# One set of spreading products for two attention blocks, and a closing barrier moved ahead of the last projections

## The chip, the cores and the metric

The kernel runs on one core of one Trainium2 chip. Its engines are named as in the profile: PE (TensorE, matrix products; PEld are its weight loads), DVE (VectorE), ACT (ScalarE), POOL (GpSimd) and SP (Sync). The metric is the device time of one execution in microseconds. The six runs of before that stand beside the changed kernel's agree within 0.14% (1321.99 to 1323.73). Two numbers are kept apart: the *time* of a run, which is the metric, and its *span*, from the first to the last instruction of the program. The time is longer than the span, by 1.3 to 1.5 us in most runs of before, and here that difference turns out to matter. All runs quoted are listed as fast; a few of them are one to two us longer than the rest, and they are named where they occur.

## The reference, cut to what matters

Two decode-attention blocks, each for one query token, are computed and their outputs laid side by side. Block A has 32 heads with 32768 keys of its own for each head; block B has 32 query heads on 8 key/value heads and looks at the last 4096 keys only.

```python
q = (x @ wq).reshape(B, Sq, H, Dh)...                 # x is one row of 512
scores = jnp.einsum("bhqd,bhkd->bhqk", q, k_cache) * (Dh ** -0.5)
p = softmax(scores)
o = jnp.einsum("bhqk,bhkd->bhqd", p, v_cache)
out = o.reshape(B, Sq, H * Dh) @ wo                   # wo is 4096 x 512
# a: all 32768 keys, 32 KV heads;  b: last 4096 keys, 8 KV heads, each for 4 query heads
return jnp.concatenate([a, b], axis=-1)
```

Nearly all the bytes are A's key and value caches, 256 MiB each in bf16, and each is read once.

## The kernel before

The program is recorded as a list of operations for each engine and then emitted inside one block. The block ends with a barrier of all five engines. Behind it the Sync engine waits for the two output stores.

```python
def build(self):
    ...
    with nc.Block() as block:                  # its end is a barrier of all five engines
        block.gpsimd(self.emit("pool"))
        block.vector(self.emit("dve"))
        block.scalar(self.emit("act"))
        block.sync(self.emit("sp"))
        block.tensor(self.emit("pe"))
    for n in self.X:
        nc.sync.wait_ge(self.outsem[n], 16)    # both outputs have landed
```

B is computed first, then A's 32 heads in a loop. "Spreading" means normalising a block's 32 x 128 attention outputs and turning them, with four small products, into the 128 x 32 layout that the output projection takes as its weights.

```python
def plan(self):
    ...
        self.emit_PV("B", g)
    self.emit_spread("B")                      # B's spread, before A's loop
    for g in range(NQH):
        ...                                    # A: load, transpose, scores, softmax, PV
    ...                                        # load_wo: the last loads, wo of B and A in pieces
    self.emit_spread("A")
    self.emit_proj()

def emit_spread(self, name):
    ...
    ri = self.op("dve", ... reciprocal(t["rinv"], ps[0:32, DH:DH + 1]), self.gath)
    ob = self.op("dve", ... tensor_scalar_mul(t["ob"], ps[0:32, 0:DH], t["rinv"]), ri)
    def mm(e):
        for dq in range(4):
            inst = e.matmul(p2[:, 0:32], lhsT=self.spread[:, 128 * dq:128 * dq + 128],
                            rhs=t["ob"][:, 32 * dq:32 * dq + 32], ...)
        return inst
    o = self.op("pe", mm, ob, self.k_sel)
    t["ozop"] = self.op("dve", ... tensor_copy(t["oz"], p2[:, 0:32]), o)
```

A's wo is loaded in six pieces of 11, 8, 6, 4, 2 and 1 rows (`WO_CUTS`), so that the last piece to land leaves little work. `emit_proj` does B's projection, sums its four strips on DVE and ACT, stores B's output, does A's projection piece by piece, evicts it in two halves (DVE and ACT) and stores A's output.

## Time and profile before

| what | before |
|---|---|
| time, 3 runs | 1322.05 us (1322.04 to 1322.24) |
| span | 1320.81 us |
| DMA moved, mean rate | 570.59 MB, 432 GB/s |
| last piece of wo landed | 1318.85 us |
| A's output store issued | 1319.70 us |
| store's semaphore complete | 1320.79 us |
| closing barrier released | 1320.36 to 1320.42 us |

The profile of before is of one more run, of 1323.17 us, which is one of the long ones: its span is that of the others, but it spent 2.36 us outside the span, where the usual is 1.3.

The page of before, first its totals, then the row of DMA in 40 slices (tenths of full business), then its queue table (packets, MB, share of the 16 engines):

```profile
span 1320.8 us, 28798 instructions
PE 968.0 (73%) x13248; PEld 677.4 (51%) x13248; DVE 753.3 (57%) x1342; ACT 56.4 (4%) x170; POOL 2.7 (0%) x22
...
DMA  9999999999999999999999999999999999999998
...
q1 hardware_dynamic: 13060, 570.43, 99.9%
q8 instruction: 8, 0.13, 0.0%
```

DMA is the limit from beginning to end. PE and DVE have time to spare everywhere but behind the last load. The end of the chain of waits of before (start, length, what) says what that last stretch is:

```profile
1288.46 29.46 DMA kbuf<-in_A_wo_dram
1317.92 0.04 issue
1317.97 1.22 PE psPT L718 x13
1319.18 0.02 issue
1319.20 0.41 DVE out_sb L725
```

And the tail of before in the timeline (start, length, engine, line, what; in brackets the engine's idle time ahead of it and what ended it):

```profile
1309.88 0.41 PE L682 MATMUL psG<-oc_A,hw 128*32 128x128 f32 x2 [1.64 <-DVE oc_A L671]
1310.32 0.16 DVE L692 RECIPROCAL rinv_A<-psG 32x1 f32<-32x1 f32 x1 [0.50 <-PE psG L682]
...
1311.24 1.90 PE L730 MATMUL psS<-kbuf,oz_B 128*1 128x512 bf16 x32
...
1314.82 1.04 PE L718 MATMUL psPT<-kbuf,oz_A 128*1 128x256 bf16 x16 [0.48 <-DMA kbuf<-in_A_wo_dram]
...
1316.73 0.82 PE L718 MATMUL psPT<-kbuf,oz_A 128*1 128x256 bf16 x12 [0.87 <-DMA kbuf<-in_A_wo_dram]
...
1317.97 1.21 PE L718 MATMUL psPT<-kbuf,oz_A 128*1 128x256 bf16 x14 [0.42 <-DMA kbuf<-in_A_wo_dram]
...
1319.20 0.41 DVE L725 CAST out_sb<-psPT 1x256 bf16<-1x256 f32 x1 [2.56 <-PE psPT L718]
...
1319.70 0.25 SPq L762 DMA_DIRECT2D out_dram<-out_sb  x1
```

The first row is the last product of A's loop, called the last gather below. Three times PE stands idle until a piece of wo has landed. A tail that starts later eats these idle times first.

The barrier is not among these rows, because semaphore instructions do not count as busy, but the trace has its records (start in us; a drain is the instruction with which an engine arrives at the barrier):

```
before   1318.90 PE drains      1319.22 DVE, 1319.25 ACT drain   1320.00 Sync drains (after its store's issue)
         1320.24 GpSimd gathers 1320.36 Sync released            1320.44 Sync waits for the store
         1320.79 store's semaphore complete                      1320.81 end of the wait = end of the span
```

So before's closing barrier runs while the store is under way.

### The profile page before, as it was taken

The page shows a single profiled execution, that of the slowest core. Times are in us where ns is not written, and L with a number is a line of the kernel's source. Part 1 is how long each engine was busy: PE and PEld are TensorE (multiplying, and loading weights), DVE is VectorE, ACT ScalarE, POOL GpSimd, SP SyncE. Part 2 cuts the span into 40 slices and gives each one's busy share as a digit, 9 for nine tenths or more (in the row PEclk, how much of TensorE's full clock was granted, in tenths as well). Part 3 has the DMA queues.
Part 4 walks back from the last instruction along what each step waited for, and adds up shares of the span by engine and source line. Part 5 has one row for each costly group of instructions (what it writes and reads, how often), then busy time and mean ns, then how long its engine had stood idle before and what let it go on. Part 6 is the DMA issues. An engine that isn't in the chain of part 4 may idle for free. (4 is left out here: it accounts for less than half of the span.)

```text
span 1320.8 us, 28798 instructions
## 1 busy us (share of the span) xinstructions
PE 968.0 (73%) x13248; PEld 677.4 (51%) x13248; DVE 753.3 (57%) x1342; ACT 56.4 (4%) x170; POOL 2.7 (0%) x22
## 2 busy tenths in 40 slices
PE   4675678777667877777787767778776767877687
PEld 3453445555444555444455544455554445555454
DVE  3563556665455666545566654566655546665564
ACT  0000000000000000000000000000000000000000
POOL 0000000000000000000000000000000000000000
PEclk8886888887788888778988887898888789888888
DMA  9999999999999999999999999999999999999998
GB/s 404 434 435 432 441 431 435 437 431 435 435 435 437 431 435 439 429 437 437 429 437 439 429 435 439 429 435 439 429 439 437 427 441 435 429 439 435 429 439 371
DMA packets 13359, 570.59 MB, mean 432 GB/s; under 512 B 1570, under 2 KB 1700, under 8 KB 2084
## 3 DMA queue, kind: packets, MB, share of 16 engines
q1 hardware_dynamic: 13060, 570.43, 99.9%
q8 instruction: 8, 0.13, 0.0%
q10 hardware_dynamic: 288, 0.00, 0.0%
q14 instruction: 3, 0.02, 0.0%
HBM read 570.43 MB, written 0.00 MB: 432 GB/s over the span
## 5 line engine op out<-in xcount | busy, mean ns | idle before, releaser
L556 DVE COPY kt<-psT 128x1024 bf16<-128x1024 bf16 x1056 | 656.2, 684 | 238.1 <-PE psT L552 236.3
L552 PE MATMUL psT<-ident,kbuf 128*128 128x128 bf16 x8448 | 582.3, 235 | 167.8 <-DMA kbuf<-in_A_k_cache_dram 154.2
L552 PEld LDWEIGHTS psT<-ident,kbuf 128*128 128x128 bf16 x8448 | 542.7, 107 | 260.0 <-DMA kbuf<-in_A_k_cache_dram 162.3
L655 PE MATMUL psACC<-vbuf,ptsb 128*4 128x512 bf16 (+1 forms) x2112 | 185.4, 527 | 22.8 <-ACT ptsb L630 22.0
L575 PE MATMUL psS<-kt,qw 128*32 128x512 bf16 x2048 | 158.3, 386 | 14.7 <-DVE kt L556 14.7
L669 DVE TENSOR_SCALAR oc_A<-psACC,hot_A 128x128 f32<-128x128 f32 x32 | 11.2, 351 | 249.9 <-PE psG L682 249.9
L655 PEld LDWEIGHTS psACC<-vbuf,ptsb 128*4 128x4 bf16 (+1 forms) x2112 | 59.4, 111 | 139.1 <-issue 91.0
L603 ACT ACTIVATE psb<-psS,nb_A 128x512 bf16<-128x512 f32 x32 | 22.0, 687 | 1168.0 <-DVE nb_A L602 1168.0
L575 PEld LDWEIGHTS psS<-kt,qw 128*32 128x32 bf16 x2048 | 34.1, 95 | 57.4 <-DVE kt L556 30.6
L682 PE MATMUL psG<-oc_A,hw 128*32 128x128 f32 (+1 forms) x128 | 19.3, 227 | 52.3 <-DVE oc_A L671 52.3
L682 PEld LDWEIGHTS psG<-oc_A,hw 128*32 128x32 f32 x128 | 11.4, 109 | 62.5 <-DVE oc_A L671 55.0
L627 PE MATMUL psPT<-ident,psb 128*128 128x128 bf16 x136 | 18.0, 275 | 34.0 <-ACT psb L603 34.0
L671 DVE SCALAR_TENSOR_TENSOR oc_A<-psACC,hot_A,oc_A 128x128 f32<-128x128 f32 x96 | 33.7, 351 | 3.4
L592 DVE TENSOR_REDUCE tr_in<-psS 128x1 f32<-128x512 f32 x34 | 23.5, 692 | 17.8 <-PE psS L575 17.8
L627 PEld LDWEIGHTS psPT<-ident,psb 128*128 128x128 bf16 x136 | 10.2, 117 | 37.0 <-ACT psb L603 36.7
L596 PE MATMUL psACC<-rows,tr_in 128*1 128x64 f32 x64 | 8.8, 220 | 25.6 <-DVE tr_in L592 25.6
L630 ACT ACTIVATE ptsb<-psPT 128x512 bf16<-128x512 bf16 x34 | 20.3, 597 | 31.1 <-PE psPT L627 31.1
L596 PEld LDWEIGHTS psACC<-rows,tr_in 128*1 128x1 f32 x64 | 2.7, 81 | 35.7 <-DVE tr_in L592 35.7
L600 PE MATMUL psACC<-mr_A,nscale 1*128 1x1 f32 x64 | 12.3, 259 | 9.8 <-DVE mr_A L599 9.8
L600 PEld LDWEIGHTS psACC<-mr_A,nscale 1*128 1x128 f32 x64 | 9.6, 186 | 15.8 <-DVE mr_A L599 15.8
L602 DVE COPY nb_A<-psACC 128x1 f32<-128x1 f32 x32 | 5.1, 158 | 15.2 <-PE psACC L600 15.2
L599 DVE TENSOR_REDUCE mr_A<-psACC 1x1 f32<-1x64 f32 x32 | 6.8, 213 | 11.8 <-PE psACC L596 11.8
(78 smaller groups left out, 71.7 us busy)
## 6 DMA issues: line engine op xcount, KB each, us to landing
kbuf<-in_A_k_cache_dram SPq DMA_DIRECT2D x4, 4096.0 KB, 22.6
kbuf<-in_B_k_cache_dram SPq DMA_DIRECT2D x2, 4096.0 KB, 31.7
vbuf<-in_B_v_cache_dram SPq DMA_DIRECT2D x2, 4096.0 KB, 25.1
vbuf<-in_B_wq_dram SPq DMA_DIRECT2D x1, 4096.0 KB, 12.4
vbuf<-in_A_wq_dram SPq DMA_DIRECT2D x1, 4096.0 KB, 32.0
kbuf<-in_B_wo_dram SPq DMA_DIRECT2D x2, 2048.0 KB, 32.2
kbuf<-in_A_wo_dram SPq DMA_DIRECT2D x1, 1408.0 KB, 25.2
kbuf<-in_A_wo_dram SPq DMA_DIRECT2D x1, 1024.0 KB, 27.3
```

The source lines that it names most:

```text
L552: inst = e.transpose(T[:, 128 * k:128 * k + 128], src[:, DH * k:DH * k + DH], self.ident[:, :])
L556: self.copies.append(self.op("dve", lambda v: v.tensor_copy(KT[:, :], T[:, :]), o, to="pe"))
L575: inst = e.matmul(self.S[32 * c:32 * c + 32, :], lhsT=win, rhs=self.kt[(bb + c // 2) % NKT][:, 512 * (c % 2):512 * (c % 2) + 512], start=b ...
L592: o = dve(lambda v: v.reduce_max(tr["in"][:, 0:1], self.S[:, :], axis=AXX), self.sdone, self.k_pool, to="pe" if name == "A" else None)
L596: o = self.op("pe", lambda e: e.matmul(self.ACC[0:1, 0:64], lhsT=tr["in"][:, 0:1], rhs=self.rows64[:, :], start=True, stop=True, skip_grou ...
L600: o = self.op("pe", lambda e: e.matmul(self.ACC[:, 64:65], lhsT=self.nscale[:, :], rhs=t["mr"][0:1, :], start=True, stop=True, skip_group_ ...
L603: self.sread = self.op("act", lambda s: s.activation(out=self.psb[:, :], in_=self.S[:, :], func=ACTF.Exp, bias=t["nb"][:, k:k + 1], scale= ...
L627: inst = e.transpose(PT[:, 128 * jj:128 * jj + 128], self.psb[:, 128 * jj:128 * jj + 128], self.ident[:, :])
L630: self.ptread = self.op("act", lambda s: s.activation(out=self.ptsb[:, :], in_=PT[:, 0:512], func=ACTF.Copy), self.psread, to="pe")
L655: inst = e.matmul(acc[32 * c:32 * c + rows, 0:512], lhsT=lhsT, rhs=rhs, start=begin, stop=end, tile_position=(0, 32 * c), skip_group_check ...
L671: o = self.op("dve", lambda v, src=src, hot=hot: v.scalar_tensor_tensor(out=oc, in0=src, scalar=hot, in1=oc, op0=ALU.mult, op1=ALU.add), p ...
L682: return self.op("pe", lambda e: e.matmul(self.G[0:32, c0 + c:c0 + c2], lhsT=win, rhs=t["oc"][g % len(t["oc"])][:, c:c2], start=False, sto ...
```

## The change

The intent is twofold. B is only normalised before A's loop; one set of four spreading products, 64 columns wide, then does both blocks at the end, which saves four products and a copy. And the operations behind the loop ("tail") are emitted after the block, so that its barrier stands ahead of the last projections instead of behind them. Cut to its core:

```diff
     def build(self):
...
             block.tensor(self.emit("pe"))
+        for eng, e in dict(pe=nc.tensor, dve=nc.vector, act=nc.scalar, sp=nc.sync).items():
+            self.rest[eng](e)
         for n in self.X:
             nc.sync.wait_ge(self.outsem[n], 16)
...
     def emit(self, eng):
-        ops = self.prog[eng]
+        ops = [o for o in self.prog[eng] if not o.tail]
+        tail = [o for o in self.prog[eng] if o.tail]
...
+            self.rest[eng] = lambda e: straight(e, tail, seen, base)
...
-        self.emit_spread("B")
+        self.emit_norm("B")
...
-        self.emit_spread("A")
+        self.tail = True
+        self.emit_spread()
         self.emit_proj()
...
+    def emit_spread(self):
+        ob, p2 = self.ob, self.T[0]
+        o = self.emit_norm("A")
         def mm(e):
             for dq in range(4):
-                inst = e.matmul(p2[:, 0:32], ..., rhs=t["ob"][:, 32 * dq:32 * dq + 32],
+                inst = e.matmul(p2[:, 0:64], ..., rhs=ob[:, :].rearrange("p (n x) -> p n x", n=2)[:, :, 32 * dq:32 * dq + 32],
...
-        deps = (self.wosem[name][part], 16), self.c[name]["ozop"]
+        deps = (self.wosem[name][part], 16), self.ozop
```

A consequence: B's projections, which needed nothing of A, now wait for A's normalisation, products and copy.

## The prediction

> **What bounds the kernel.** DMA. The queue table gives 99.9% of the span of 16 DMA engines to the load queue (570.43 MB, 432 GB/s); the 40-slice rows show DMA at 9 tenths in all slices but the last. PE is busy 73% and DVE 57%. The chain that ended last confirms it: 29.46 us of DMA for the last pieces of A's output weights (the last lands at 1318.85), then 1.22 us of last products (line 718), 0.41 us of DVE eviction, and the output store, issued from 1319.70 to 1319.95. The span ends at 1320.81. So only the 2 us behind the last landing can be won.

> **What stands at that end.** The barrier's records are in the trace, though not in the busy rows: engines drain (PE 1318.90, DVE and ACT by 1319.68, SP 1320.00 to 1320.21), GpSimd gathers at 1320.24, all are released by 1320.44. Sync then waits for the store's semaphore, which comes at 1320.79, 1.09 us after its issue (the other store took 1.13 us). The closing barrier is thus already hidden under the store. [...]

> **What the change removes.** B's spread: 4 products, 1 copy and their semaphores, about 1 us of PE and DVE before A's loop, with DMA saturated: worth 0. The barrier between store issue and final wait: the wait still ends with the store: worth 0 to 0.1 us.

> **What it adds and moves.** The barrier now sits between loop and tail. PE is its last arrival: its loop-end branch is done at 1311.0, then a branch and a drain, then 0.2 us from last gather to release (as at the end of before). I estimate the reciprocal at 1311.6 instead of 1310.32. B's projections, which started at 1311.24, must now also wait for A's normalisation, products and copy: about 1312.8 (estimate, +1.5 us). PE's work behind that, by issue times of before: B 1.4 to 1.5 us, A's first 22 products 1.3, next 16 0.75; PE is level at about 1316.4, just before the third A piece lands (1316.69). PE sat idle for DMA 0.48, 0.87 and 0.42 us ahead of these pieces; that slack absorbs the delay. Summing B's strips ends near 1318.2 instead of 1316.65, before DVE's last eviction at 1319.20; B's store lands near 1319.3, before A's. Nothing of this reaches the critical path.

> **Prediction.** 1322.0 us, 8 in 10 between 1321.6 and 1322.5. Faster by over 2%: 0.003; within 2%: 0.99; slower by over 2%: 0.007. If it moves at all, I expect under 0.3 us.

> **What the profile would show.** Right: DMA saturated, last landing within 0.3 us of 1318.9; the first tail DVE instruction about 1.3 us later against the loop's end; PE's idle for DMA shrunk or gone before the second and third A piece, still there before the last; 1.1 us from last store issue to final wait. Wrong: PE's last product well after the last landing (delay not absorbed), or a span end under 1.0 us after the last store's issue (barrier was on the path).

> **What would make it wrong.** [...] Time outside the span: other engines finish earlier and could shorten what follows. A DMA rate that differs between runs.

## The result

| | before | changed |
|---|---|---|
| time, median of 6 runs | 1322.05 us (1321.99 to 1323.73) | 1322.36 us (1322.26 to 1323.24) |
| span of the profiled run | 1320.81 us | 1320.67 us |

The ratio is 1.0001 with a 95% interval of 0.9988 to 1.0014: the same at 2%. The prediction of 1322.0 (1321.6 to 1322.5) held. The medians differ by 0.31 us, a hair more than the "under 0.3 us" that it allowed. Leaving out the one long run of each side (1323.73 and 1323.24), all runs of the changed kernel (1322.26 to 1322.52) lie above all runs of before (1321.99 to 1322.24), although the profiled span is a little shorter. That is small, but it is a question.

The page of the changed kernel:

```profile
span 1320.7 us, 28789 instructions
PE 966.1 (73%) x13244; PEld 675.0 (51%) x13244; DVE 751.7 (57%) x1341; ACT 56.4 (4%) x170; POOL 2.7 (0%) x22
...
DMA  9999999999999999999999999999999999999998
...
q1 hardware_dynamic: 13060, 570.43, 99.9%
```

Four products and one DVE instruction are gone, as planned, and DMA is as full as it was. The end of its chain of waits:

```profile
1286.73 31.65 DMA kbuf<-in_A_wo_dram
1318.38 0.04 issue
1318.42 0.62 PE psPT L731 x5
1319.04 0.02 issue
1319.06 0.41 DVE out_sb L738
```

The same three steps end the program. Its tail in the timeline:

```profile
1307.73 0.41 PE L689 MATMUL psG<-oc_A,hw 128*32 128x128 f32 x2 [1.64 <-DVE oc_A L678]
1309.20 0.16 DVE L696 RECIPROCAL rinv_A<-psG 32x1 f32<-32x1 f32 x1 [1.52 <-PEq L102]
...
1310.48 2.70 PE L743 MATMUL psS<-kbuf,oz 128*1 128x512 bf16 x32 [0.41 <-DVE oz L712]
...
1312.95 3.17 PE L731 MATMUL psPT<-kbuf,oz 128*1 128x256 bf16 x38
...
1316.54 0.82 PE L731 MATMUL psPT<-kbuf,oz 128*1 128x256 bf16 x12 [0.41 <-DMA kbuf<-in_A_wo_dram]
...
1317.77 1.25 PE L731 MATMUL psPT<-kbuf,oz 128*1 128x256 bf16 x14 [0.41 <-DMA kbuf<-in_A_wo_dram]
...
1319.06 0.41 DVE L738 CAST out_sb<-psPT 1x256 bf16<-1x256 f32 x1 [2.39 <-PE psPT L731]
...
1319.55 0.25 SPq L775 DMA_DIRECT2D out_dram<-out_sb  x1
```

From PE's last gather to the reciprocal it is now 1.47 us (1309.20 - 1307.73) instead of 0.44, with the releaser "PEq L102", the barrier. From there to B's first product it is 1.28 us (1310.48 - 1309.20) instead of 0.92. B's products take longer too: 2.70 us against 1.90 (the granted clock was 0.57 in 1311 to 1314 us against 1.00, see below). And the idle time ahead of the piece of 16 products is gone: the 38 products at 1312.95 run through. But ahead of the last two groups PE still waits 0.41 us for DMA each time, so nothing of the delay has come through. The loop also ended 2.15 us earlier in this execution than in the trace of before (1307.73 against 1309.88); the control below, the same kernel as before, has its last gather at 1308.17, so this varies between runs of one kernel.

### The profile page after: what moved, and what is told of

Same layout as the page of the kernel before. It is cut to its first block, busy times and chain, and to the rows that moved or that the text cites. A ratio compares the mean times of both kernels' runs of the same rounds, so it can differ in the third digit from the quotient of the medians.

```text
span 1320.7 us, 28789 instructions
## 1 busy us (share of the span) xinstructions
PE 966.1 (73%) x13244; PEld 675.0 (51%) x13244; DVE 751.7 (57%) x1341; ACT 56.4 (4%) x170; POOL 2.7 (0%) x22
## 3 DMA queue, kind: packets, MB, share of 16 engines
q1 hardware_dynamic: 13060, 570.43, 99.9%
HBM read 570.43 MB, written 0.00 MB: 432 GB/s over the span
```

## The experiments

Twelve kernels were run, with runs of before in between. All gave correct results. "Extra" below is time minus span of a run, which comes from the list of single runs (spans are listed to 0.1 us).

### Control and the two halves of the change

The control is before itself. Of the two halves, spread_only is one line away from the changed kernel, and barrier_only is before with the changed kernel's tail machinery (not repeated here) and that same line:

```diff
 # spread_only: the changed kernel without the tail
-        self.tail = True
```

```diff
 # barrier_only: before with the tail machinery
+        self.tail = True
         self.emit_spread("A")
```

> The kernel before, unchanged, as a control: it gives the spread of two equal kernels in the same rounds, and its own time outside the span. Both theories: ratio to before 1.0000 within 0.0002 (0.3 us), span 1320.6 to 1320.9 us, time minus span as in the other kernels (the changed kernel showed 1.6 us in all its runs).

> The changed kernel, unchanged. Theory (the change is off the critical path; the 0.3 us between the medians of the first measurement is spread or the chip): within 0.3 us of the control, span 1320.6 to 1320.9. Rival (the change costs 0.3 us outside the span, in what follows the last instruction): again 0.2 to 0.4 us above the control, at the same span, with a larger time minus span.

> The one set of spreading products for both blocks, without the move of the barrier: one line taken from the changed kernel. Theory: within 0.3 us of the control, because DMA is saturated where B's products are saved and B's projections, which must now wait for A's spread, start only 0.4 to 0.6 us later with 1 us and more of slack ahead of the last pieces. Rival (if the 0.3 us of the changed kernel is real): 0 if the barrier carries it, +0.3 us if the merged spread does.

> The barrier ahead of the tail, with B's spread where it was in the kernel before. Theory: within 0.3 us of the control; the reciprocal comes about 1.2 us later against PE's last gather, and the last products still start within 0.1 us of the last landing. Rival (if the 0.3 us of the changed kernel is real): +0.3 us if the barrier carries it, 0 if the merged spread does.

| kernel | median time, 5 runs | spans | extra, median |
|---|---|---|---|
| before in the same rounds (9 runs) | 1322.17 | 1320.7 to 1321.1 | 1.32 |
| before_again | 1322.06 | 1320.6 to 1320.8 | 1.36 |
| after_again | 1322.49 | 1320.7 to 1321.5 | 1.66 |
| spread_only | 1322.55 | 1320.7 to 1320.9 | 1.75 |
| barrier_only | 1322.15 | 1320.6 to 1321.0 | 1.25 |

My theory, that the 0.3 us were spread, fell. The 95% intervals of the four ratios, some 0.0028 wide, do not separate the kernels, but the extra does: run by run, spread_only has 1.67 to 1.78 us and after_again 1.59 to 1.69; before has 1.30 to 1.50 and barrier_only 1.22 to 1.40, each with one run at 2.4 to 2.5 that is dealt with in the last section. The halves add up: the merged spread costs about 0.4 us outside the span, the moved barrier saves about 0.1 us outside the span, and the sum is the +0.3 us of the changed kernel. Inside the span both are worth nothing, as predicted.

The trace shows where. Around the end of the span and behind it, it records steps of semaphore 2, which no instruction of the kernel touches: nine steps, then 228 to 249 other semaphores updated once each, then nine steps. In us from the end of the span:

```
                first nine steps                                       last nine steps
before_again   -0.16 -0.13 0.08 0.12 0.15 0.25 0.28 0.32 0.37     1.16 1.19 1.23 1.27 1.30 1.40 1.44 1.47 1.52
spread_only    -0.15 -0.12 0.09 0.13 0.16 0.26 0.29 0.33 0.37     1.16 1.20 1.24 1.28 1.30 1.80 1.84 1.87 1.92
barrier_only   -1.44 -1.09 -1.05 -1.01 0.12 0.16 0.20 0.23 0.28   1.07 1.10 1.14 1.19 1.21 1.31 1.35 1.38 1.43
after_again    -1.44 -1.09 -1.05 -1.01 0.12 0.16 0.20 0.23 0.28   1.07 1.11 1.15 1.19 1.21 1.71 1.75 1.78 1.83
```

The records do not say which engine makes a step. As I read them, the first nine go on as the five engines end their streams: with the barrier moved four of them come 1.44 to 1.01 us ahead of the span's end, for the other engines (in the trace of the changed kernel at 1319.24 to 1319.67, where PE's last product ends at 1319.03 and the evictions at 1319.47), and only Sync is waited for, so the nine are through 0.28 us behind the span instead of 0.37. That is the 0.1 us. With the merged spread, one of the last nine steps (the sixth) comes 0.49 or 0.50 us behind the fifth instead of 0.10. That is the 0.4 us.

### Which engine's instruction stream carries the 0.4 us

The merged spread takes four instructions from PE's stream and one from DVE's. Each was put back by itself, with work whose result nobody reads:

```diff
 # after_pe4                                     # after_dve1
-        self.emit_norm("B")                     +        pad = ...alloc_sbuf_tensor("pad", [128, 32], BF16)
+        o = self.emit_norm("B")                 +        self.op("dve", lambda v: v.tensor_copy(pad[:, :],
+        self.op("pe", pad, o, self.k_sel)       +                self.ident[:, 0:32]), self.k_ident)
 # pad: B's four old products into an unread corner of PSUM
```

> The changed kernel with B's four old spreading products put back on PE, their result unread; so PE has as many instructions as in before, DVE one fewer. So far: kernels with the merged spread spend 1.6 to 1.75 us outside the span, those without 1.25 to 1.35, and the records behind the span show one gap of 0.5 us in place of 0.1 [...]. Theory P (what counts is how many instructions PE's stream has, thus where its end code lies): time minus span falls back to 1.25 us, the gap to 0.1 us, the median to about 1322.0. Theory D (DVE's stream): stays at 1.65 us. Theory M (something about the merged spread itself): stays at 1.65 us. Span 1320.6 to 1320.9 in all.

> The changed kernel with one unused DVE copy put in where B's copy of the spread was; DVE has as many instructions as in before, PE four fewer. Theory P (PE's stream): time minus span stays at 1.65 us, median about 1322.4. Theory D (DVE's stream): falls to 1.25 us, median about 1322.0. Theory M: stays.

| kernel | PE, DVE instructions against before | median time | spans | extra, median (range) | fifth to sixth step |
|---|---|---|---|---|---|
| after_pe4 | 0, -1 | 1322.51 | 1320.7 to 1321.1 | 1.67 (1.61 to 1.77) | 0.49 |
| after_dve1 | -4, 0 | 1322.27 | 1320.7 to 1321.3 | 1.27 (1.21 to 1.29) | 0.10 |
| before, same rounds (9 runs) | 0, 0 | 1322.44 | 1320.8 to 1321.2 | 1.38 | |

Theory D it is. One DVE instruction of no use, put in ahead of A's loop, takes the 0.4 us away again. So it is neither the merged product nor PE's stream, but DVE's stream. That what counts is where this stream ends is inferred, because only one added instruction at one place was tried. Other kernels have other DVE counts with the barrier moved: +1 (after_late2) gave an extra of 1.39 us, +2 (barrier_late2) gave 1.52, +7 (after_late8) gave 1.22. That is no trend, as one would expect of a position and not of an amount of work. With +2 the sixth step is on time (0.10 us); there an 8 KB packet, which the profile lists under the kind "instruction", moves behind the span and ends last (more on this under "More barriers"). The four traces in which DVE has two or more instructions more than before, barrier instructions counted, have such an 8 KB packet in their last 2 us or behind the span, and the other ten have none, which points at a position too. What exactly delays the sixth step is not shown. One trace (four more barriers, below) has DVE pausing between two bare barrier instructions, 0.51 us from its release to its next drain against 0.11 us in the barriers before it, with nothing to wait for; the size fits, the cause stays open.

### How much slack the tail has

Two or eight DVE copies were put ahead of the reciprocal, which makes the whole tail later. I had estimated 0.7 us for each; in the traces the reciprocal came 1.2 us later with two of them (1312.15, where the first copy starts at 1310.94) and 4.8 us later with eight:

```diff
 # after_late2, after_late8, barrier_late2: in the tail, ahead of A's normalisation
+        for i in range(2):                      # 8
+            self.op("dve", lambda v, i=i: v.tensor_copy(self.kt[4 + i % 4], self.T[3] as bf16))
```

> The changed kernel with two unneeded DVE copies of 0.68 us between the barrier and the reciprocal: the whole tail behind the barrier comes 1.4 us later. Theory (the tail is off the critical path; PE has 1 to 3 us of slack before the last landing, depending on when the loop ends and which clock is granted): span up by 0 to 0.3 us. Rival (the tail is on the path): span up by 1.4 us.

> The same with eight such copies: the tail comes 5.7 us later. Theory: the slack is used up and the rest surfaces, span up by 2.5 to 4.5 us, and PE no longer waits for any of the last pieces. Rival (the tail is on the path): up by 5.7 us. Rival (these steps never matter): 0.

> The barrier moved, B's spread left where it was, and the same two needless DVE copies as in after_late2 between barrier and reciprocal. Theory S (the merged spread takes the slack: B's projections wait for A's whole spread, and all traces with it show the clock at half for 3.4 to 6.9 us inside the tail, the three without it at full): span up by 0 to 0.3 us here, against 1.3 to 1.6 us in after_late2. Rival L (the slack is lost because the loop itself ended 1.7 us later in that run): up by 1 us or more here too.

| kernel | spans, 4 runs | before in the same rounds |
|---|---|---|
| after_late2 | 1322.1, 1322.1, 1322.3, 1322.4 | 1320.8 to 1321.2 |
| after_late8 | 1323.8, 1324.7, 1325.0, 1326.2 | 1320.8 to 1321.2 |
| barrier_late2 | 1320.7, 1320.8, 1320.8, 1320.9 | 1320.6 to 1320.9 |

My expectation for after_late2 was wrong and the rival's was right: 1.2 us of delay raised the span by 1.2 us (from a median of 1321.0 to one of 1322.2). So in these four runs the changed kernel's tail had no slack to speak of, although its first trace shows PE waiting for DMA. With eight copies, 4.8 us of delay cost 2.8 to 5.2 us against the same median (3.85 in the median, as expected, but one run lies above my range); what was absorbed varies by 2.4 us among four runs. And barrier_late2, with the same delay but B's spread done early, pays nothing in any of its four runs. So with the barrier moved and B's spread left in its place there were at least 1.2 us of slack, and in the four runs of after_late2 there were not. The two ran on different chips, and no run excludes the chip as a rival.

The two timelines, after_late2 first:

```profile
1309.47 0.41 PE L689 MATMUL psG<-oc_A,hw 128*32 128x128 f32 x2 [1.63 <-DVE oc_A L678]
...
1313.42 3.56 PE L747 MATMUL psS<-kbuf,oz 128*1 128x512 bf16 x32 [0.41 <-DVE oz L716]
1316.78 3.68 PE L735 MATMUL psPT<-kbuf,oz 128*1 128x256 bf16 x64
...
1320.99 0.25 SPq L779 DMA_DIRECT2D out_dram<-out_sb  x1
```

```profile
1308.05 0.41 PE L689 MATMUL psG<-oc_A,hw 128*32 128x128 f32 x2 [1.64 <-DVE oc_A L678]
...
1311.51 3.58 PE L739 MATMUL psS<-kbuf,oz_B 128*1 128x512 bf16 x32
...
1314.88 4.30 PE L727 MATMUL psPT<-kbuf,oz_A 128*1 128x256 bf16 x64
...
1319.71 0.25 SPq L771 DMA_DIRECT2D out_dram<-out_sb  x1
```

In after_late2 all 64 of A's products run without a wait for DMA, and the last starts at 1320.19, while the last piece had landed at 1318.79: PE, not DMA, sets the end. B's first product comes 3.95 us behind the last gather (1313.42 - 1309.47) against 3.46 us (1311.51 - 1308.05), so the merged spread accounts for 0.49 us of the difference. The other 1.42 us is that A's loop ended later in this run. The spans of all four runs of after_late2 agree, so I cannot call that chance, nor did any run show a reason for it; how the slack splits between merged spread and loop end stays open. In the 14 traces the last gather starts between 1307.08 and 1309.88 us, and it is as late as here (1309.47) or later in before, before_plus1_barriers and quarters_barrier too.

A second thing had not been in the prediction: the granted clock. The stretches of 3 us in the tail (PE busy, PEld, DVE, ACT and POOL busy, then the clock, DMA share, GB/s), first of before, then of spread_only:

```profile
1311.00:1314.00 3.00, 2.94 (x56) 1.78 (x58) 0.88 (x2) 0.08 (x1) 0.00 (x0) 1.00 0.99 416
1314.00:1317.00 3.00, 1.65 (x30) 0.88 (x26) 2.04 (x3) 1.10 (x2) 0.00 (x0) 1.00 0.99 406
```

```profile
1311.00:1314.00 3.00, 3.00 (x32) 1.08 (x26) 0.15 (x1) 0.00 (x0) 0.00 (x0) 0.50 0.99 417
1314.00:1317.00 3.00, 3.00 (x42) 2.06 (x38) 2.28 (x4) 1.18 (x2) 0.00 (x0) 0.67 0.98 400
```

### More barriers at the end of before

```diff
 # before_plus1_barriers, before_plus4_barriers
             block.tensor(self.emit("pe"))
+        for _ in range(1):                      # 4
+            with nc.Block():
+                pass
```

> The kernel before with one more empty barrier behind its closing one, ahead of the wait for the store; one barrier takes 0.35 to 0.45 us from Sync's drain to release. Theory (the closing barrier is hidden under the store, which lands 0.35 us after the release): span up by 0 to 0.15 us. Rival (the barrier is on the path): up by 0.35 to 0.45 us.

> The same with four more barriers. Theory: the first is hidden, the rest surfaces: span up by 4 x 0.4 minus 0.35, so 1.0 to 1.4 us, and the final wait ends at once when it starts. Rival (each is on the path): up by 1.4 to 1.8 us.

| kernel | median time, 4 runs | spans | extra, median |
|---|---|---|---|
| before, same rounds (9 runs) | 1322.14 | 1320.6 to 1320.9 | 1.38 |
| before_plus1_barriers | 1322.80 | 1320.6 to 1321.1 | 1.97 |
| before_plus4_barriers | 1324.19 | 1322.1 to 1322.3 | 1.94 |

In the span the expectation held both times: one more barrier is still hidden under the store (the trace has Sync released from it at 1320.71 and the store complete at 1320.81), and of four more 1.4 us come through. The second is partly luck: one of the four took 0.78 us from release to release, with DVE's pause in it, against 0.33 to 0.36 us for the other three. But the time of before_plus1_barriers rose by 0.66 us, nearly all of it in the extra. So "hidden under the store" was only half right: Sync waits for the store in any case, but the other four engines have to get through the barrier before their streams end, and that shows outside the span. In the records the first nine steps end 0.70 us behind the span instead of 0.37, which is 0.33 us, just what the added barrier takes from release to release. The other 0.3 us fits a record of DMA: an instruction packet of 8 KB moved from 1.75 to 2.20 us behind the span, later than the last step at 1.83. Over all 14 traces the extra of the profiled run follows from what comes last. In eleven it is the last step's time less 0.16 to 0.19 us. In the three where an instruction packet ends later (before, barrier_late2 and before_plus1_barriers, at 2.65, 1.81 and 2.20 us) it is that packet's end less 0.29 us (2.36, 1.52 and 1.91). The extra barrier also says why moving the barrier gains only 0.1 us: it ended early enough that the other engines were late by only that much.

### A version meant to beat both

```diff
 # quarters_barrier: barrier_only with A's projection in four strips of 128 columns
-            inst = e.matmul(bank[64 * i:64 * i + 1, 0:256], ..., rhs=rhs[:, 256 * i:256 * i + 256], ...)   # i = 0, 1
+            inst = e.matmul(bank[32 * i:32 * i + 1, 0:128], ..., rhs=rhs[:, 128 * i:128 * i + 128], ...)   # i = 0..3
-        out, src = self.out_sb[0:1, 256 * i:256 * i + 256], bank[64 * i:64 * i + 1, 0:256]
+        out, src = self.out_sb[64 * i:64 * i + 64, :], bank[64 * i:64 * i + 64, 0:128]
-        e.dma_start(self.out[0, :, 0:512], self.out_sb[:, :])
+        e.dma_start(self.out[0, :, 0:512].rearrange("a (c x) -> (a c) x", c=4), self.out_sb[0:128:32, :])
```

> A version meant to beat both: barrier moved, B's spread as in before, and A's last products in four strips of 128 columns in place of two of 256, so that DVE and ACT each evict 128 columns (estimate from 0.41 us for 256 and 0.69 us for 512 columns: 0.28 us) and the store takes four pieces of 256 B. Theory: span down by 0.1 to 0.15 us and 0.1 us less outside it, median about 1321.9 against 1322.1 to 1322.4 of before. Rival (the store of four pieces takes longer to be received, or the smaller products start more slowly): no gain. A gain under 0.15 us can drown in the runs' spread; then the trace's steps from the last landing to the end decide.

It did not beat them: a median of 1322.50 us against 1322.14, spans of 1321.1, 1321.2, 1321.2, 1322.7 and 1322.8 us. The profiled run is one of the two long ones; its end in the timeline, and its line of instruction packets:

```profile
1318.44 0.28 PE L725 MATMUL psPT<-kbuf,oz_A 128*1 128x128 bf16 x8 [0.19 <-DMA kbuf<-in_A_wo_dram]
...
1320.36 0.27 PE L725 MATMUL psPT<-kbuf,oz_A 128*1 128x128 bf16 x4 [1.63 <-DMA kbuf<-in_A_wo_dram]
1320.67 0.28 DVE L732 CAST out_sb<-psPT 64x128 bf16<-64x128 f32 x1 [3.56 <-PE psPT L725]
1320.71 0.27 ACT L733 ACTIVATE out_sb<-psPT 64x128 bf16<-64x128 f32 x1 [5.12 <-PE psPT L725]
1321.07 0.62 SPq L769 DMA_DIRECT2D out_dram<-out_sb  x1
```

```profile
q8 instruction: 9, 0.15, 0.0%
```

The eviction did shrink from 0.41 to 0.28 us, as estimated. But the store of four pieces took 0.62 us to issue instead of 0.25, and 1.65 us from issue to semaphore instead of 1.09, which costs more than that. And there are nine instruction packets instead of eight, with 64 products more in the program: one more packet of 16 KB was moved from 1318.32 to 1319.29. Fifteen of the 16 increments of the last piece of wo had come by 1318.74; the sixteenth came at 1320.31. Its last packets moved only at 1319.27 and 1319.38, when the instruction packet ended. The trace does not name the DMA engine of a packet, but the times leave little else: an instruction packet in the wrong place delayed the last load by 1.5 us. That is inferred from these times, not shown.

The fastest version measured is no clear winner. barrier_only has a median 0.02 us below that of before (extra 1.25 against 1.32 us). after_dve1, the changed kernel with its one useless DVE instruction, lies 0.17 us below (extra 1.27 against 1.38 us). Both differences are within the runs' spread.

## Why the prediction was right or wrong

- *DMA bounds the kernel, only the stretch behind the last landing counts.* Right: DMA stands at 9 tenths in both, and the same three steps end both chains.
- *The barrier was hidden under the store, worth 0 to 0.1 us.* Right in size: 0.1 us, and it lies outside the span. The reason given was only half of it. In the span the barrier was hidden (one more barrier changes nothing there), but the end of the other engines' streams counted, by 0.09 us in the records (the first nine steps through at 0.28 instead of 0.37 us).
- *B's spread before the loop: "worth 0".* This is the step that failed, though the total stayed in the range. Its products and their time were worth 0, but the one DVE instruction that went with them changed DVE's stream (by where it ends, as inferred above) and cost 0.4 us outside the span. after_dve1 shows it: the instruction put back, the 0.4 us gone. That the total stayed in the range is partly luck: a missing term of 0.4 us, less the 0.1 us gained, still fits into 0.45 us on either side of before's median.
- *The tail comes later: reciprocal +1.3 us, B's projections +1.5 us.* Nearly right. Against the last gather the reciprocal came 1.03 us later (1.47 instead of 0.44 us) and B's first product 1.39 us later (2.75 instead of 1.36 us).
- *PE's slack absorbs it.* Right for the profiled run, and too generous as a rule. The prediction took B's products at 1.4 to 1.5 us of PE time; at the half clock that was granted they took up to 3.6 us. A further delay of 1.2 us came through whole. The spans of single runs fit with that: before's go up to 1321.2 us, the changed kernel's to 1321.6, 1321.5 and 1321.3 in three of its eleven runs. No trace of those long runs exists, so that last link is an inference.
- *What would make it wrong: "time outside the span: other engines finish earlier and could shorten what follows".* The place was right and the sign of the sum was not: -0.1 us for the engines' earlier end, +0.4 us for DVE's stream.

## What to carry to other kernels

When a kernel is bound by DMA to its last byte, taking work from PE and DVE in mid-program can be worth nothing in the span, as here, and what remains to be won or lost are tenths of a microsecond in the last 2 us and behind them; there, one instruction more or less in an engine's stream weighed more than the work taken away. So compare the time minus the span of every run, and before explaining a few tenths by the change itself, add a useless instruction to one engine and see whether the difference goes away. And test slack by spending it: a delay of known size in the tail tells more than idle times read from one trace, in which the loop may have ended early or the clock been full.

## What else the traces show

- One DVE instruction more or less moved the time outside the span from 1.66 us (after_again) to 1.27 us (after_dve1).
- In quarters_barrier a 16 KB instruction packet took 0.97 us, and, as inferred above from the times of the packets, it held up the data queued behind it, so that the last load landed 1.5 us late. Single long runs may have the same cause: before, before_again and barrier_only have some with 2.3 to 3.0 us outside the span instead of 1.3. In the one of these that was profiled (before, 2.36 us), a 16 KB instruction packet moved behind the span, from 1322.27 to 1323.46 us, and the trace of before_again, at 1.34 us, has none there. The other long runs left no trace.
- In before's trace the first nine steps of semaphore 2 took 0.53 us, the single updates of the other semaphores 0.80 us (1321.10 to 1321.90) and the last nine steps 0.36 us. These are the recorded steps alone.
- In before a store of 1 KB issued by Sync took 1.09 us from issue to semaphore (1319.70 to 1320.79), of which 0.72 us passed before its packet moved and 0.33 us from the packet's end to the semaphore. In quarters_barrier, issuing four pieces of 256 B instead of one of 1 KB took 0.62 us instead of 0.25.
- A window in which PE was busy for 0.38 of the time was followed by half the clock (spread_only, 1305.73 to 1309.14), and one with 0.50 was not (barrier_only, 1305.19 to 1308.61).
